# Reordering the second expert layer: copies and conversions among the next pair's sums, later ring loads, separate sum buffers

## Chip, core and metric

The program runs on one of the eight cores of a Trainium2 chip. The metric is the device time of one execution in microseconds (us). A core has TensorE (PE in the views; its weight loads are PEld), VectorE (DVE), ScalarE (ACT), GpSimd (POOL) and SyncE (SP). Each runs its own instructions in order and waits at semaphores for the others. Here SP issues nearly all DMAs.

## What is computed

Causal attention with a forget gate, over 4 batches, 8 heads, 576 positions and 64 dimensions, then two dense layers over the 2304 tokens:

```python
x = attention(q, k, v, f)               # 2304 x 512
h = x @ w_in                            # 512 -> 2048
y = softplus(h) @ w_out                 # 2048 -> 512
gate = sigmoid(y @ w_gate)              # 512 -> 1536
out = (gate * (y @ w_val)) @ w2_out     # 1536 -> 512
```

Everything is float32. Each product is made of three matmuls on a high and a low part of both operands, so every operand is first split: ACT casts the high part, DVE subtracts it from the source to get the low part.

## The kernel before

There are three stages. `Attention` is not touched. `Moe1` is the softplus layer: five tiles of tokens, sixteen blocks per tile; block `fc` is 12 matmuls for `h`, the softplus, the split into `gh` and `gl`, and 12 matmuls into `oX` and `oY`, one block behind. `Moe2` is the gated layer: tiles of 512, 512, 512, 512 and 256 tokens and 12 units per tile. An even unit k makes the gate, the odd one after it the value, and the two are a pair.

A unit of `Moe2` for a 512-token tile (`hidden`, from line 807) multiplies 2x2 blocks by Strassen's scheme, seven products of six matmuls. In PE's order they are A11, S2, A12, S1, A22, S3, S4. They go into four PSUM buffers in turn (tags `s` and `t`, two each; the trace names the tiles `h_A` and `h_S`). A22 reuses the `t` buffer of S2, so it waits until DVE has read S2 (line 831). That needs ACT's copy `p1` of A11 (line 830, tile `L`). DVE makes five more sums (lines 832 to 839). Then ACT applies the sigmoid (line 841, tile `bh`), or DVE multiplies by the gate (line 843, tile `bl`). After an odd unit, `parts` (line 862) splits the product into `gh` and `gl` for two blocks, f = 0 and 1. `output` (line 874) adds these blocks' products into `zX` and `zY`, in the two units that follow. When a tile's last block is in, `leave` (line 890) copies the four sums `zX`, `zY` out and stores them. The next tile's first `output` writes the same PSUM.

Weights reach `Moe2` through DRAM. During `Moe1`, `Sums` forms the Strassen sums of the weights and stores them: high parts through the buffers `sh0` and `sh1`, low parts `l` (lines 679 to 683). `load` (line 724) reads one unit's weights, seven DMAs of 256 KB, into a ring of four places. `load_out` reads `w2_out`. `step` (line 764) prepares the next tile's tokens: it loads `yT` into `r` and `bl` (line 785), then ACT and DVE split them (lines 779, 780) and make their Strassen sums.

The order is written out by hand: each engine executes what the Python code emits, in that order. On SP a DMA waits until the buffer is free, and until the eighth DMA before it has landed. `extra1` and `after` (in the main function) set where `Moe2`'s first loads stand among `Moe1`'s last blocks: before the change, `m2.load()` is called in blocks 10 to 13 of the last tile.

Of the kernel before, what the change touches and what calls it, by code (L numbers as in the profile page):

```python
# [9 lines left out]
F32 = mybir.dt.float32  # L10
F32R = mybir.dt.float32r
# [10 lines left out]
class Attention:  # L22
# [391 lines left out]
    def run(self, others):  # L414

        edge = {0: self.START, self.NP - 1: self.END}
        ops = [(self.PERIOD * p + edge.get(p, {}).get(op, r), i, p, op) for p in range(self.NP)
               for i, (op, r) in enumerate(self.WHEN.items()) if p or op[0] not in self.FIRST]
        ops += [(t, -1, i, f) for i, (t, f) in enumerate(others)]
        for t, i, p, op in sorted(ops, key=lambda x: x[:3]):  # L420
            if i < 0:
                op()
            else:
                getattr(self, op[0])(self.R.setdefault(p, {}), p, *op[1:])
# [110 lines left out]
def three(nc, ps, terms, start, stop):  # L535

    n = len(terms)
    for i, (ah, al, bh, bl) in enumerate(terms):
        nc.tensor.matmul(ps, ah, bh, start=start and i == 0, stop=False)  # L539
        nc.tensor.matmul(ps, ah, bl, start=False, stop=False)  # L540
        nc.tensor.matmul(ps, al, bh, start=False, stop=stop and i == n - 1)  # L541


def block(w, i):
    return w[:, 128 * i:128 * i + 128]
# [90 lines left out]
class Sums:  # L636
# [11 lines left out]
    def add(self, lane, sums, names, srcs):  # L648

        for n in names:  # L650
            self.d[n] = self.dr.tile([4 if sums else 1, 2, 128, 512], F32, name="sd_%s%d" % n)
        self.lanes[lane].append((sums, names, srcs))
# [52 lines left out]
class Moe2:  # L705
# [6 lines left out]
    def __init__(self, nc, FC, yT, out, S, chain, ps, slot, zs):  # L712
# [3 lines left out]
        self.n = self.NT * 2 * self.J  # L716
        self.acc, self.g, self.x, self.loaded = {}, {}, {}, 0

    def get(self, name, i):
        if (name, i) not in self.cache:  # L720
            self.cache[name, i] = self.slot(name, i)
        return self.cache[name, i]
# [91 lines left out]
    def hidden(self, k):  # L814
        t, r = divmod(k, 2 * self.J)
        gate = r % 2 == 0
        if self.plain(t):
            return self.hidden_plain(k, t, gate)
        nc = self.nc
        A, B = self.weights(k), self.tokens(t)  # L820
        C = self.chain("G" if gate else "V", k)
        p1, u2, u3, u4 = (self.chain(n, k) for n in ("p1", "u2", "u3", "u4"))
        c = lambda i: C[:, 256 * i:256 * i + 256]

        def product(tag, a, b):
            ps = self.ps.tile([128, 512], F32, tag=tag, bufs=2, name=f"h{k}_{a}")[:, 0:256]
            three(nc, ps, [(block(A[a][0], kk), block(A[a][1], kk), *B[b][kk]) for kk in range(2)], True, True)
            return ps
        add = nc.vector.tensor_add
        nc.scalar.copy(p1, product("s", "A11", "x11"))  # L830
        add(u2, product("t", "S2", "T2"), p1)  # L831
        add(c(0), product("s", "A12", "x21"), p1)
        p5 = product("t", "S1", "T1")
        add(u4, p5, u2)
        p4 = product("t", "A22", "T4")
        add(u3, product("s", "S3", "T3"), u2)  # L836
        add(c(3), p5, u3)
        add(c(2), p4, u3)
        add(c(1), product("s", "S4", "x22"), u4)  # L839
        if gate:  # L840
            nc.scalar.activation(C, C, AF.Sigmoid)  # L841
        else:
            nc.vector.tensor_mul(C, C, self.chain("G", k))  # L843

    def hidden_plain(self, k, t, gate):
        nc = self.nc
        w = [[self.get(f"ring{k % self.RING}", 2 * f + p) for p in range(2)] for f in range(2)]
        x = [[self.get(f"x{t % 2}", 2 * (c // 2) + p)[:, 256 * (c % 2):256 * (c % 2) + 256] for p in range(2)]
             for c in range(4)]
        C, G = self.chain("G" if gate else "V", k), self.chain("G", k)  # L850
        for f in range(2):
            b = self.ps.tile([128, 512], F32, tag="ts"[gate], bufs=2, name=f"h{k}_{f}")[:, 0:256]
            three(nc, b, [(block(w[f][0], c), block(w[f][1], c), *x[c]) for c in range(4)], True, True)
            o = slice(256 * f, 256 * f + 256)
            if gate:
                nc.scalar.activation(C[:, o], b, AF.Sigmoid)
            else:
                nc.vector.tensor_mul(C[:, o], b, G[:, o])

    def parts(self, k):  # L860
        nc, m, n = self.nc, self.chain("V", k), self.TILES[k // (2 * self.J)][1]
        for f in range(2):
            s = m[:, n * f:n * f + n]
            h, l = (self.chain("g" + p, k)[:, 0:n] for p in "hl")
            nc.scalar.copy(h, s)  # L865
            nc.vector.tensor_sub(l, s, h)
            self.g[k // 2, f] = h, l


    def output(self, i, f):  # L870

        nc = self.nc
        t, j = divmod(i, self.J)
        o, n = self.TILES[t]
        first, last = (j, f) == (0, 0), (j, f) == (self.J - 1, 1)
        if first:
            X = self.ps.tile([128, 1024], F32, tag="X", name=f"zX{t}")
            Y = self.ps.tile([128, 1024], F32, tag="Y", name=f"zY{t}")
            self.acc[t] = [X[:, 0:512], X[:, 512:1024], Y[:, 0:512], Y[:, 512:1024]]
        gh, gl = self.g.pop((i, f))  # L880
        wh, wl = (self.get("w2", 2 * (2 * j + f) + p) for p in range(2))
        for b in range(n // 128):
            a = self.acc[t][b]
            nc.tensor.matmul(a, block(gh, b), wh, start=first, stop=False)  # L884
            nc.tensor.matmul(a, block(gh, b), wl, start=False, stop=False)  # L885
            nc.tensor.matmul(a, block(gl, b), wh, start=False, stop=last)
        if last:
            for b in range(2):
                self.leave(t, b)

    def leave(self, t, b):
        nc, z, o = self.nc, self.zs[b], self.TILES[t][0] + 128 * b
# [10 lines left out]
            self.load_out(k + 2)  # L903
        self.load()

    def run(self, first, before):
        for k in range(first, self.n + 2):
            if k < self.n:
                self.unit(k)
            i = (k - 2) // 2  # L910
            if k == first:
                before()
            elif i >= self.J and i % self.J == 0 and k % 2 == 0:

                for b in (2, 3):
                    self.leave(i // self.J - 1, b)
            if i >= 0:
                self.output(i, k % 2)
            if k < self.n and k % 2:
                self.parts(k)  # L920
# [11 lines left out]
def kernel(ctx: ExitStack, tc, q, k, v, f, w_in, w_out, w_gate, w_val, w2_out, out):  # L932
    nc = tc.nc
# [28 lines left out]
    with ExitStack() as actx:  # L962
# [6 lines left out]
        m1 = []  # L969
# [14 lines left out]
    chain, m1 = m1  # L984
    xb = pool("xb", 1, **later)
    x1.pools.append(xb)
    wc = pool("wc", 1, **later)
    W.add_slots(wc, tags("c", 4 * FC1 - 2 * EARLY - 2 * MORE))
    W.limit = 2 * FC1
    last = m1.n - FC1  # L990
    raws, ws, highs = [], [], [wc.tile([128, 512], F32R, name=f"sh{i}") for i in range(2)]
    S = Sums(nc, W, dr, raws, ws, highs, chain)
    gv = [(n, j, w) for j in range(FC2 // 2) for n, w in (("g", w_gate), ("v", w_val))]
    for i, (n, j, w) in enumerate(gv):
# [19 lines left out]
    box = {}  # L1014
# [18 lines left out]
    def buffers(name, k):  # L1033

        if name in ("gh", "gl"):
            return chain.tile([128, 512], F32R, tag=name, name=f"{name}{k}", bufs=2)
        if name == "r1":
            return raw.tile([128, 512], F32, tag="xr", name=f"r1_{k}")
        if name in ("p1", "u2", "u3", "u4"):
            if "L" not in box:  # L1040
                box["L"] = [chain.tile([128, 512], F32, tag="L", name=f"L2_{i}", bufs=2) for i in range(2)]
            i = ("p1", "u2", "u3", "u4").index(name)
            return box["L"][i % 2][:, 256 * (i // 2):256 * (i // 2) + 256]
        if "b" not in box:
            box["b"] = [xb.tile([128, 4, 448], F32R, tag="x" + w, name="b" + w)[:].bitcast(F32).rearrange(
                "p a b -> p (a b)") for w in "hl"]
        b = box["b"]["GqVr".index(name[0]) // 2]
        return b[:, 0:1024] if name in "GV" else b[:, 1024:1536]

    m2 = Moe2(nc, FC2, yT, out, S, buffers, ps, slot, ws)  # L1050
# [4 lines left out]
    def extra1(u):  # L1055
        t, fc = divmod(u, FC1)
        if u == FC1 - 1:
            fixed()
        if t and fc:
            if fc < 15:  # L1060
                S.step(0)
            if t < m1.NT - 1 or fc >= 4:
                S.step(1)
        if t == m1.NT - 1 and fc >= 5:
            if fc - 5 < m2.STEPS:
                m2.step(0, fc - 5)
            if fc >= 10 and fc < 14:
                m2.load()

    def after(i):  # L1070
        m2.load_out(0)
        m2.load_out(1)
        m2.unit(i)

    def rest():
        for d in (2, 3):
            m1.leave(m1.NT - 1, d)

    W.alone()
    W.tick(2)  # L1080
    m1.run(len(UNITS), pieces1, extra1, after)
    m2.run(m1.LAG, rest)


# [32 lines left out]
```

## Time and profile before

| | |
|---|---|
| three runs | 1073.56, 1077.10, 1076.71 us; median 1076.71 us |
| the profiled execution | 1076.53 us, of which the span from the first to the last instruction is 1074.7 us |
| PE busy | 1033.5 us, 96% of the span |
| DVE, ACT, POOL busy | 679.0, 452.6, 155.6 us |
| mean granted clock of TensorE | 0.988 |
| attention, the softplus layer, the gated layer | to about 300 us, to about 633 us, to the end |

All times below count from the start of the span. "Idle before" is an engine's own idle time just ahead of an instruction, with what ended it. A PE matmul is shown with a modelled end, so successive matmuls overlap in the rows; how many PE does in a time is read from their starts.

### The profile page before, as it was taken

The numbers are of one execution on the slowest core, as the hardware profiler recorded it, in microseconds if no ns is written. First come the engines' busy times: TensorE is split into PE (matmuls) and PEld (weight loads), VectorE is DVE, ScalarE is ACT, GpSimd is POOL, SyncE is SP. The second block draws the span as 40 slices with busy tenths as digits, with TensorE's granted clock in tenths as the row PEclk, the third lists the DMA queues.
The fourth block names the chain that finished last, engine by engine and source line by source line (L and its number), as shares of the span: only waits on it lengthen the run. The fifth ranks groups of instructions, "written<-read, shape, count | busy, mean of one in ns | idle before, by whom it ended". The sixth has DMA issues, their size and how long they took to land.

```text
span 1074.7 us, 17922 instructions
## 1 busy us (share of the span) xinstructions
PE 1033.5 (96%) x6376; PEld 925.0 (86%) x6376; DVE 679.0 (63%) x1453; ACT 452.6 (42%) x989; POOL 155.6 (14%) x158
## 2 busy tenths in 40 slices
PE   4989999989999999999999998999999999999998
PEld 3777888868889999999999988998999899989997
DVE  6898999978945755656646636655655656555421
ACT  4687888865644343343344432222212222122121
POOL 7656776550000000000000000000000000000000
PEclk8899999999999999999999999999999999999999
DMA  6354454455534654655643599988787887786481
GB/s 169 89 150 129 126 142 125 138 142 176 212 123 174 197 211 175 213 191 182 226 170 138 182 394 371 327 263 272 245 252 245 274 261 231 254 257 210 152 271 63
DMA packets 129493, 218.24 MB, mean 203 GB/s; under 512 B 16174, under 2 KB 46526, under 8 KB 129404
## 3 DMA queue, kind: packets, MB, share of 16 engines
q1 hardware_dynamic: 129244, 216.80, 62.3%
q8 instruction: 50, 0.82, 0.3%
q10 hardware_dynamic: 160, 0.30, 0.1%
q14 instruction: 39, 0.32, 0.1%
HBM read 171.21 MB, written 45.83 MB: 202 GB/s over the span
## 4 chain that ended last, share of the span: by engine, by line
PE 85%; DVE 7%; DMA 4%; ACT 2%; issue 2%; SPq 0%; POOL 0%; DVEq 0%; POOLq 0%; ACTq 0%
PE h L541 7%; PE h L539 7%; PE h L540 7%; PE s L220 5%; PE t L250 4%; PE x L322 4%; PE h_S L539 4%; PE h_S L541 4%; PE h_S L540 4%; PE h_A L539 3%; PE h_A L541 3%; PE h_A L540 3%; PE zX L884 2%; PE zX L885 2%; PE oY L539 2%; PE oY L541 2%
## 5 line engine op out<-in xcount | busy, mean ns | idle before, releaser
L541 PE MATMUL h<-xh,wi_l 128*128 128x448 f32 (+1 forms) x320 | 119.0, 372 | 0.0
L540 PE MATMUL h<-xl,wi_h 128*128 128x448 f32 (+1 forms) x320 | 119.0, 372 | 0.0
L539 PE MATMUL h<-xh,wi_h 128*128 128x448 f32 (+1 forms) x320 | 118.9, 372 | 0.0
L581 DVE TENSOR_TENSOR gl<-L,gh 128x448 fp32r<-128x448 f32 (+1 forms) x80 | 51.1, 638 | 102.6 <-ACT gh L580 102.4
L569 ACT ACTIVATE L<-h 128x448 f32<-128x448 f32 (+1 forms) x80 | 44.2, 552 | 148.6 <-PE h L541 144.9
L865 ACT CAST gh<-bl 128x512 fp32r<-128x512 f32 (+1 forms) x60 | 32.2, 577 | 142.8 <-DVE bl L843 120.5
L232 ACT ACTIVATE P<-P,m 128x128 f32<-128x128 f32 (+3 forms) x144 | 83.4, 583 | 13.0 <-DVE m L227 13.0
L540 PE MATMUL h_S<-x,ring 128*128 128x256 f32 x288 | 81.5, 283 | 0.0
L227 DVE CUSTOM_DVE_ANT_0 P<-s,mask 128x256 f32<-128x256 f32 (+3 forms) x144 | 70.8, 517 | 16.4 <-PE s L220 11.2
L539 PE MATMUL h_S<-x,ring 128*128 128x256 f32 x264 | 74.7, 283 | 0.0
L541 PE MATMUL h_S<-x,ring 128*128 128x256 f32 x264 | 74.7, 283 | 0.0
L841 ACT ACTIVATE bh<-bh 128x1024 f32<-128x1024 f32 x24 | 25.4, 1059 | 107.8 <-DVE bh L839 107.8
L250 PE MATMUL t<-ident,P 128*128 128x128 f32 x400 | 62.3, 293 | 8.6 <-DVE PTbl L272 5.6
L541 PEld LDWEIGHTS h<-xh,wi_l 128*128 128x128 f32 x320 | 60.1, 188 | 7.2
L539 PEld LDWEIGHTS h<-xh,wi_h 128*128 128x128 f32 x320 | 60.1, 188 | 7.1
L540 PEld LDWEIGHTS h<-xl,wi_h 128*128 128x128 f32 x320 | 60.1, 188 | 7.1
L250 PEld LDWEIGHTS t<-ident,P 128*128 128x128 f32 x400 | 47.0, 147 | 21.1 <-DVE PTbl L272 7.1
L681 DVE TENSOR_TENSOR l<-fw,sh 128x512 fp32r<-128x512 f32 x60 | 40.7, 686 | 37.9 <-ACT sh L680 37.9
L540 PEld LDWEIGHTS h_S<-x,ring 128*128 128x128 f32 x288 | 55.2, 192 | 0.0
L540 PE MATMUL h_A<-x,ring 128*128 128x256 f32 x192 | 54.3, 283 | 0.0
L539 PE MATMUL h_A<-x,ring 128*128 128x256 f32 x168 | 48.5, 289 | 5.2 <-DVE L L831 4.0
L836 DVE TENSOR_TENSOR L<-h_S,L 128x256 f32<-128x256 f32 x48 | 20.4, 425 | 49.7 <-PE h_S L541 49.7
(233 smaller groups left out, 3065.3 us busy)
## 6 DMA issues: line engine op xcount, KB each, us to landing
ring<-sd_g SPq DMA_DIRECT2D x192, 256.0 KB
ring<-sd_v SPq DMA_DIRECT2D x192, 256.0 KB
raw_wi<-in_moe_w_in_dram SPq DMA_DIRECT2D x16, 512.0 KB
raw_wo<-in_moe_w_out_dram SPq DMA_DIRECT2D x16, 512.0 KB
fraw<-in_moe_w_gate_dram SPq DMA_DIRECT2D x12, 512.0 KB
fraw<-in_moe_w_out_dram SPq DMA_DIRECT2D x12, 512.0 KB
sd_g<-sh SPq DMA_DIRECT2D x24, 256.0 KB
sd_g<-l SPq DMA_DIRECT2D x24, 256.0 KB
```

Source lines behind the costliest of these rows:

```text
L220: nc.tensor.matmul(ps[h][:, 0:N], L[o], r[o, 0:N], start=j == 0, stop=j == n - 1)
L227: self.nc.vector.tensor_tensor_reduce(P, src, mask, -0.125, 3e38, op0=ALU.add, op1=ALU.min, accum_out=R["m"][:, t:t + 1])
L232: self.nc.scalar.activation(P, P, AF.Exp, bias=R["m"][:, t:t + 1], scale=-1.0, accum_out=R["sum"][:, t:t + 1])
L250: nc.tensor.transpose(ps[:, 128 * n:128 * n + 128], R["P"][:, o:o + 128], self.ident)
L322: nc.tensor.matmul(R["acc%d" % h][:, o:o + n], v, t[:, col:col + n], start=j == 0 and w == 0, stop=j == 1 and w == 1)
L539: nc.tensor.matmul(ps, ah, bh, start=start and i == 0, stop=False)
L540: nc.tensor.matmul(ps, ah, bl, start=False, stop=False)
L541: nc.tensor.matmul(ps, al, bh, start=False, stop=stop and i == n - 1)
L569: nc.scalar.activation(g, ph, AF.Softplus)
L581: nc.vector.tensor_sub(gl, s, gh)
L681: nc.vector.tensor_sub(l, w[n], h)
L865: nc.scalar.copy(h, s)
```

## The change

It has five parts. (1) In `parts` the second block's split goes onto a list `between[0]` and is emitted in the middle of the next unit, after the adds of lines 831 and 832. (2) The four `leave` of a tile go onto `between[0]` and `between[1]`, so they are emitted inside the next tile's unit: two after line 832, two after line 839. The last two copies of the softplus layer (`rest`) go the same way. (3) `m2.load()` is called in blocks 13, 14 and 15 and once in `after`, instead of blocks 10 to 13. (4) `p1` and `u2` to `u4` move from two `L` buffers of the softplus layer to `sh0` and `sh1`, buffers of `Sums`. (5) ACT's table for the sigmoid is loaded explicitly at the start of `after`.

```diff
--- before.py
+++ after.py
@@ -716,6 +716,8 @@
         self.n = self.NT * 2 * self.J
         self.acc, self.g, self.x, self.loaded = {}, {}, {}, 0
 
+        self.between = [[], []]
+
     def get(self, name, i):
         if (name, i) not in self.cache:
             self.cache[name, i] = self.slot(name, i)
@@ -830,6 +832,7 @@
         nc.scalar.copy(p1, product("s", "A11", "x11"))
         add(u2, product("t", "S2", "T2"), p1)
         add(c(0), product("s", "A12", "x21"), p1)
+        self.other(0)
         p5 = product("t", "S1", "T1")
         add(u4, p5, u2)
         p4 = product("t", "A22", "T4")
@@ -837,10 +840,16 @@
         add(c(3), p5, u3)
         add(c(2), p4, u3)
         add(c(1), product("s", "S4", "x22"), u4)
+        self.other(1)
         if gate:
             nc.scalar.activation(C, C, AF.Sigmoid)
         else:
             nc.vector.tensor_mul(C, C, self.chain("G", k))
+
+    def other(self, i):
+        for f in self.between[i]:
+            f()
+        self.between[i] = []
 
     def hidden_plain(self, k, t, gate):
         nc = self.nc
@@ -851,6 +860,7 @@
         for f in range(2):
             b = self.ps.tile([128, 512], F32, tag="ts"[gate], bufs=2, name=f"h{k}_{f}")[:, 0:256]
             three(nc, b, [(block(w[f][0], c), block(w[f][1], c), *x[c]) for c in range(4)], True, True)
+            self.other(f)
             o = slice(256 * f, 256 * f + 256)
             if gate:
                 nc.scalar.activation(C[:, o], b, AF.Sigmoid)
@@ -859,12 +869,18 @@
 
     def parts(self, k):
         nc, m, n = self.nc, self.chain("V", k), self.TILES[k // (2 * self.J)][1]
-        for f in range(2):
+
+        def part(f):
             s = m[:, n * f:n * f + n]
             h, l = (self.chain("g" + p, k)[:, 0:n] for p in "hl")
             nc.scalar.copy(h, s)
             nc.vector.tensor_sub(l, s, h)
             self.g[k // 2, f] = h, l
+        part(0)
+        if k + 1 < self.n:
+            self.between[0].append(lambda: part(1))
+        else:
+            part(1)
 
 
     def output(self, i, f):
@@ -885,8 +901,12 @@
             nc.tensor.matmul(a, block(gh, b), wl, start=False, stop=False)
             nc.tensor.matmul(a, block(gl, b), wh, start=False, stop=last)
         if last:
-            for b in range(2):
-                self.leave(t, b)
+            if t < self.NT - 1:
+                for b in range(4):
+                    self.between[b // 2].append(lambda b=b: self.leave(t, b))
+            else:
+                for b in range(n // 128):
+                    self.leave(t, b)
 
     def leave(self, t, b):
         nc, z, o = self.nc, self.zs[b], self.TILES[t][0] + 128 * b
@@ -903,17 +923,11 @@
             self.load_out(k + 2)
         self.load()
 
-    def run(self, first, before):
+    def run(self, first):
         for k in range(first, self.n + 2):
             if k < self.n:
                 self.unit(k)
             i = (k - 2) // 2
-            if k == first:
-                before()
-            elif i >= self.J and i % self.J == 0 and k % 2 == 0:
-
-                for b in (2, 3):
-                    self.leave(i // self.J - 1, b)
             if i >= 0:
                 self.output(i, k % 2)
             if k < self.n and k % 2:
@@ -988,7 +1002,7 @@
     W.add_slots(wc, tags("c", 4 * FC1 - 2 * EARLY - 2 * MORE))
     W.limit = 2 * FC1
     last = m1.n - FC1
-    raws, ws, highs = [], [], [wc.tile([128, 512], F32R, name=f"sh{i}") for i in range(2)]
+    raws, ws, highs = [], [], [wc.tile([128, 512], F32R, tag=f"sh{i}", name=f"sh{i}") for i in range(2)]
     S = Sums(nc, W, dr, raws, ws, highs, chain)
     gv = [(n, j, w) for j in range(FC2 // 2) for n, w in (("g", w_gate), ("v", w_val))]
     for i, (n, j, w) in enumerate(gv):
@@ -1038,7 +1052,7 @@
             return raw.tile([128, 512], F32, tag="xr", name=f"r1_{k}")
         if name in ("p1", "u2", "u3", "u4"):
             if "L" not in box:
-                box["L"] = [chain.tile([128, 512], F32, tag="L", name=f"L2_{i}", bufs=2) for i in range(2)]
+                box["L"] = [wc.tile([128, 512], F32, tag=f"sh{i}", name=f"L2_{i}") for i in range(2)]
             i = ("p1", "u2", "u3", "u4").index(name)
             return box["L"][i % 2][:, 256 * (i // 2):256 * (i // 2) + 256]
         if "b" not in box:
@@ -1064,22 +1078,21 @@
         if t == m1.NT - 1 and fc >= 5:
             if fc - 5 < m2.STEPS:
                 m2.step(0, fc - 5)
-            if fc >= 10 and fc < 14:
+            if fc >= 13:
                 m2.load()
 
     def after(i):
+        nc.scalar.preload_act_table_set("sigmoid_and_others")
+        m2.load()
         m2.load_out(0)
         m2.load_out(1)
         m2.unit(i)
-
-    def rest():
-        for d in (2, 3):
-            m1.leave(m1.NT - 1, d)
+        m2.between = [[lambda: m1.leave(m1.NT - 1, 2), lambda: m1.leave(m1.NT - 1, 3)], []]
 
     W.alone()
     W.tick(2)
     m1.run(len(UNITS), pieces1, extra1, after)
-    m2.run(m1.LAG, rest)
+    m2.run(m1.LAG)
 
 
 # ---- launch: one core; inputs and outputs as the reference has them ----
```

PE's rows are the same, in the same order. Three places elsewhere are moved.

On SP, at the end of the softplus layer, from the token load of the first tile on. `sd_g<-sh` and `sd_g<-l` are stores of `Sums`; `ring` are weight loads for the gated layer. Before:

```order
L785 DMA bl<-yT 128x512
L733 DMA ring_0_6593<-sd_g_3411 128x512
L733 DMA ring_1_6595<-sd_g_3411 128x512
L733 DMA ring_2_6597<-sd_g_3411 128x512
L733 DMA ring_3_6599<-sd_g_3411 128x512
L733 DMA ring_4_6601<-sd_g_3411 128x512
L733 DMA ring_5_6603<-sd_g_3411 128x512
L739 DMA ring_6_6605<-sd_g_3411 128x2x256
L682 DMA sd_g_3433<-sh_3409 128x512
L683 DMA sd_g_3433<-l_7_1_1_6638 128x512
L733 DMA ring_0_6649<-sd_v_3412 128x512
```

The same place after the change:

```order
L787 DMA bl<-yT 128x512
L682 DMA sd_g_3433<-sh_3409 128x512
L683 DMA sd_g_3433<-l_7_1_1_6624 128x512
L682 DMA sd_g_3433<-sh_3409 128x512
L683 DMA sd_g_3433<-l_7_1_2_6706 128x512
L735 DMA ring_0_6716<-sd_g_3411 128x512
L735 DMA ring_1_6718<-sd_g_3411 128x512
```

Four stores, of which the last pair is made in block 13, now stand ahead of the first ring load. From that load to the token load `bl<-yT` of the second tile, later in the same queue, there are 61 DMAs before and 57 after.

On ACT, the units 1 to 3 of the gated layer, with `L608` the late copy of the softplus layer's `oY`. Before:

```order
L830 COPY L_0_6859<-h_A_6946 128x256
L608 COPY fw_4131<-oY_6209 128x448
L865 CAST gh_7019<-bl 128x512
L865 CAST gh_7023<-bl 128x512
L830 COPY L_0_6859<-h_A_7030 128x256
L841 ACTIVATE bh<-bh 128x1024
L779 CAST y1h<-bl 128x512
L830 COPY L_0_6859<-h_A_7118 128x256
```

After:

```order
L832 COPY L_0_6860<-h_A_6947 128x256
L608 COPY fw_4131<-oY_6209 128x448
L876 CAST gh_7020<-bl 128x512
L832 COPY L_0_6860<-h_A_7027 128x256
L876 CAST gh_7051<-bl 128x512
L845 ACTIVATE bh<-bh 128x1024
L781 CAST y1h<-bl 128x512
L832 COPY L_0_6860<-h_A_7119 128x256
```

The second block's cast goes behind `p1` of unit 2. In both orders the cast `y1h<-bl` of the newly loaded tokens stands ahead of `p1` of unit 3 (the last row).

On DVE, the first unit of the second tile, with `zX` and `zY` the copies of the first tile's sums. Before:

```order
L843 TENSOR_TENSOR bl<-bl,bh 128x1024
L893 COPY fw_4128<-zX_7099 128x512
L866 TENSOR_TENSOR gl_8067<-bl,gh_8066 128x512
L866 TENSOR_TENSOR gl_8071<-bl,gh_8070 128x512
L831 TENSOR_TENSOR L_1_6860<-h_S_8085,L_0_6859 128x256
L832 TENSOR_TENSOR bh<-h_A_8093,L_0_6859 128x256
L834 TENSOR_TENSOR L_1_6860<-h_S_8101,L_1_6860 128x256
```

After:

```order
L847 TENSOR_TENSOR bl<-bl,bh 128x1024
L877 TENSOR_TENSOR gl_8064<-bl,gh_8063 128x512
L833 TENSOR_TENSOR L_1_6861<-h_S_8078,L_0_6860 128x256
L834 TENSOR_TENSOR bh<-h_A_8086,L_0_6860 128x256
L913 COPY fw_4128<-zX_7100 128x512
L877 TENSOR_TENSOR gl_8099<-bl,gh_8098 128x512
L837 TENSOR_TENSOR L_1_6861<-h_S_8102,L_1_6861 128x256
```

The copy of `zX` and one subtraction go from ahead of the first two sums to behind them. On ACT the copy of `zY` likewise goes from behind the sigmoid to ahead of it.

## Rows read from the trace of the kernel before

**Rows 1.** PE's waits from 560 us to the end: engine, line, releaser: total, times, longest

```profile
PE h_A L539 <- DVE L L831: 4.3, 5, 2.5
PE zY L884 <- ACT fw L893: 3.3, 3, 1.1
PE h_A L539 <- ACT L L569: 1.1, 1, 1.1
```

**Rows 2.** Timeline of PE, units 0 to 3: start, duration, line, tiles, [idle before <-releaser]

```profile
633.23 0.39 PE L539 MATMUL h_A<-x,ring 128*128 128x256 f32 x1 [1.07 <-ACT L L569]
...
634.65 0.28 PE L541 MATMUL h_S<-x,ring 128*128 128x256 f32 x1
635.04 0.38 PE L539 MATMUL h_A<-x,ring 128*128 128x256 f32 x1
...
650.39 0.39 PE L539 MATMUL h_A<-x,ring 128*128 128x256 f32 x1 [2.54 <-DVE L L831]
...
658.03 0.28 PE L540 MATMUL h_S<-x,ring 128*128 128x256 f32 x1
658.15 0.28 PE L541 MATMUL h_S<-x,ring 128*128 128x256 f32 x1
659.37 0.38 PE L539 MATMUL h_A<-x,ring 128*128 128x256 f32 x1 [0.95 <-DVE L L831]
```

**Rows 3.** Timeline of SP, from the last sums' stores to the second tile's token load

```profile
608.12 0.38 SPq L682 DMA_DIRECT2D sd_v<-sh  x1
...
610.19 2.82 SPq L733 DMA_DIRECT2D ring<-sd_g  x6
...
651.34 0.53 SPq L785 DMA_DIRECT2D bl<-yT  x1
```

**Rows 4.** Timeline of ACT in the same stretch

```profile
618.94 0.57 ACT L580 CAST gh<-L 128x448 fp32r<-128x448 f32 x1
...
631.81 0.62 ACT L680 CAST sh<-fw 128x512 fp32r<-128x512 f32 x1 [7.34 <-DMA sd_g<-sh]
...
656.84 0.62 ACT L779 CAST y1h<-bl 128x512 fp32r<-128x512 f32 x1 [2.07 <-DMA bl<-yT]
```

**Rows 5.** Timeline of DVE in the same stretch

```profile
620.44 0.69 DVE L681 TENSOR_TENSOR l<-fw,sh 128x512 fp32r<-128x512 f32 x1 [0.28 <-ACT sh L680]
...
658.90 0.42 DVE L831 TENSOR_TENSOR L<-h_S,L 128x256 f32<-128x256 f32 x1
```

**Rows 6.** Stretches: length, busy time of the engines, granted clock, DMA share, GB/s

```profile
605.00:610.00 5.00, 5.00 (x26) 4.54 (x25) 3.59 (x7) 2.19 (x5) 0.00 (x0) 1.00 0.44 165
...
640.00:650.00 10.00, 7.85 (x66) 7.64 (x64) 5.84 (x12) 3.29 (x7) 0.00 (x0) 1.00 1.04 382
```

**Rows 7.** Two stretches in attention, the same columns: PE first

```profile
89.50:92.90 3.40, 1.45 (x10) 0.97 (x11) 3.37 (x11) 1.03 (x4) 0.01 (x1) 1.00 0.95 283
92.93:96.34 3.41, 3.41 (x17) 2.64 (x17) 1.94 (x5) 2.83 (x9) 0.64 (x1) 0.50 0.08 20
```

**Rows 8.** Timeline of PE, unit 8 and the first change of tiles

```profile
698.86 0.39 PE L539 MATMUL h_A<-x,ring 128*128 128x256 f32 x1 [0.28 <-DVE L L831]
...
745.58 0.28 PE L541 MATMUL h_S<-y1l,ring 128*128 128x256 f32 x1
745.82 0.39 PE L539 MATMUL h_A<-y1l,ring 128*128 128x256 f32 x1
...
750.72 0.50 PE L884 MATMUL zY<-w,gh 128*128 128x512 f32 x1 [1.09 <-ACT fw L893]
```

**Rows 9.** Timeline of DVE and ACT at the first change of tiles

```profile
744.14 1.29 DVE L866 TENSOR_TENSOR gl<-bl,gh 128x512 fp32r<-128x512 f32 x2 [1.17 <-ACT gh L865]
...
749.02 0.68 DVE L893 COPY fw<-zY 128x512 f32<-128x512 f32 x1
...
750.10 0.57 ACT L893 COPY fw<-zY 128x512 f32<-128x512 f32 x1
```

## The prediction

> **What bounds the kernel now.** I read the table of engines first: PE is busy 96% of the span and its order is unchanged, so the time can only change where PE waits, or runs at another clock. Next come PE's waits in the second half [rows 1]: 8.7 us in nine waits. Three are for ACT's copy of `zY`, five for DVE's line 831, one for the softplus. In the timeline of PE [rows 2] the first four stand close together, in units 0, 2 and 3 of the gated layer; three show 1.07, 2.54 and 0.95 us of idle time, and the one at 635.04 shows as a late start. A shown wait costs more than it shows. Successive matmuls start 0.12 us apart (658.03, 658.15), and the next, at 659.37, starts 1.10 us later than that pace, where 0.95 us is shown; so 0.16 us is added for each (at 635.04 the start is 0.27 late). The matmul after a wait runs about 0.10 us longer (0.38 against 0.28). The four together cost 1.07 + 2.54 + 0.95 + 3 x 0.16 + 0.27 + 4 x 0.10 = 5.7 us.
>
> Then I ask what ends these waits. In the timeline of ACT [rows 4] the cast `sh` stood 7.34 us idle until the store of its buffer had landed, and the softplus of the last block is behind it. Later the cast `y1h` waited for the token load `bl`, and unit 3's `p1` is behind that. PE went on at 659.37, 2.53 us after `y1h` began. Both releasers are DMAs. In the timeline of SP [rows 3] the first ring load is issued at 610.19 and `bl` at 651.34. By the stretches [rows 6] the 16 DMA engines went from a share of 0.44 before 610 us to 1.04 at 640 to 650 us, with 382 GB/s. The queue is full, so landing times are set by how many DMAs stand ahead. There are 61 DMAs from the first ring load to `bl`, in 41.15 us, which is 0.675 us each.
>
> **The later ring loads (part 3).** The stores no longer stand behind ring loads, so the 7.34 us wait of ACT goes, and with it PE's waits in unit 0. What is late next is `bl`. The first ring load now stands behind the stores of block 13. In that block `gh` ends at 619.51 [rows 4], the cast takes 0.62 and the subtraction 0.69 us, which ended at 621.13 even with a short wait in front [rows 5]; the load follows at about 621.2, that is 11.0 us later than now. From there to `bl` stand 57 DMAs, four fewer.
>
> Before, `bl` had landed 46.65 us after the first ring load was issued (656.84 less 610.19). Taking off four DMAs at 0.675 leaves 43.95, so it lands at 665.15: the late bound. Before, the first ring load also had at least four DMAs ahead of it in flight, issued from 608.12 on [rows 3]; after, the queue is nearly empty at 621 us. That takes off up to 2.7 us more: 662.45, the early bound. I take 663.4, nearer the early one, since the empty queue is read from the order and from the idle share. PE goes on 2.53 us later, at 665.93. Without any wait it would be at that matmul at 659.37 - 5.31 (the four waits) - 0.30 (three restarts) = 653.76. So one wait of 12.2 us, 12.3 with its restart, takes the place of 5.7: +6.6 us (5.6 to 8.3 by the two bounds).
>
> The Trainium skill (DMA: Bandwidth & Descriptors, Specifications) states about 358 GB/s as a core's share of its memory. By that figure 57 loads of 256 KB take an estimated 41.7 us rather than 57 x 0.675 = 38.5, and the sum would be 3.2 us higher. The trace disagrees with the figure (382 GB/s).
>
> **The clock after that wait.** PE has had no wait near 12 us in this half of the trace. The nearest rows are in attention [rows 7]: after a stretch in which PE was busy 1.45 of 3.40 us, the granted clock was 0.50 (1.2 instead of 2.4 GHz) for 3.41 us with PE busy throughout. That cost about half of 3.41 us, 1.7 us. I add 1.7. The bounds are 0, if it is granted in full when PE starts again, and 3.4, two such stretches. A gain is excluded, since it ran at 1.00 before.
>
> The Trainium skill (TensorE: Matmul & The Clock Gate, Part 1) says the same from the other side: half rate is what an idle engine gets, and activity releases it. By the rule the loss is certain and only its length open; by the mean clock of 0.988 alone one would have set it to nothing, and the sum at 1.7 us less.
>
> **Units 0 to 2 (parts 4 and 5, the split of unit 1, the late copies).** The table load moves from behind unit 0's sums to before `p1`. `p1` now has to wait until the last store from `sh0` has landed. In unit 2 one cast instead of two stands ahead of `p1`. I cost all of this at nothing: unit 3's wait ends at a landing, and a us won or lost in units 0 to 2 is only taken from that wait. If that cover is gone, the wait of 2.54 us in unit 2 [rows 2] shrinks to about 0.6, since one of its two casts and one copy are out of the way.
>
> **Moved splits (part 1).** In unit 8 of three tiles, DVE's line 831 stands behind two subtractions and the token sums, and PE waits 0.28 us (three of the five waits) [rows 1, 8]: 0.28 + 0.16 + 0.10 = 0.54. One subtraction takes 1.29 / 2 = 0.65 us [rows 9] and now stands behind line 832, so the wait goes: -1.6 us for three. In all other even units the moved subtraction lies in the time in which DVE waits for the fourth product. If that cover were too short, PE would lose up to 0.65 us in each.
>
> **Moved copies (part 2).** At each of three changes of tiles PE loses 0.12 + 0.10 us at 745.82 behind the copy of `zX`. Then it loses 1.09 + 0.16 = 1.25, and 0.11 for the restart, at `zY` [rows 8], because ACT's copy stands behind the sigmoid and begins at 750.10 [rows 9]. Together 4.7 us for three. After, ACT's copy runs in the middle of the unit. DVE's copy of `zY` still stands behind the last sum and ends at 749.70 [rows 9], where PE could begin at 750.72 - 1.25 = 749.47: about 0.27 + 0.10 us stay, 1.1 for three. Net -3.6 us. The bounds are 0 (`zY` as late as now) and -4.7. The stores of these copies now stand before the next ring load on SP, at most 1.5 us in its way, in a stage in which the ring is three units ahead.
>
> **Sum.** The profiled execution took 1076.53 us, 0.18 below the median of 1076.71. 1076.53 + 6.6 + 1.7 - 1.6 - 3.6 = 1079.6 us. A change of 0.3% (3.2 us), about what a measurement of this kernel can tell from none, begins at 1073.5 and at 1079.9.
>
> **Rivals.** (a) Not slower: the queue carries the 57 DMAs faster, and `bl` lands at 660. For it: the early bound has no stray delay in it. Against it: 0.675 us was held for 41 us at a full share. The wait then costs 660 + 2.53 - 653.76 + 0.10 = 8.9, net +3.2; with -5.2 and the clock kept, 1074.5 us. It decides at a landing of about 662 with the clock kept, and 660.3 with it halved; earlier than that, the gains win.
>
> (b) Much faster: the token load is no bound, because its landing before 651 us lets unit 3 pass. Then -5.7 + 0.6 - 5.2 = -10.3, 1066.2 us. For it: ACT's wait for `bl` was only 2.07 us [rows 4]. Against it: at 651 the queue would have had to do 57 DMAs in 30 us.
>
> (c) Slower: the changes of tiles keep their wait, since `zY` as one tile is released only by DVE's copy behind the last sum, and two more instructions on DVE in that unit push this back. For it: that copy ends after PE is ready. Against it: DVE had idle time in front of line 836. Only the 1.6 us are won: 1083.2 us.
>
> **Chances.** The forecast 0.55, from 1077 to 1082 by its own bounds, half of it on each side of 1079.9: 0.27 same, 0.28 slower. (a) 0.16: 0.13 same, 0.03 faster. (b) 0.09, faster. (c) 0.20: 0.02 same, 0.18 slower. Faster 0.12, same 0.42, slower 0.46. The range leaves out (b) below and the clock's 3.4 us on top of (c) above: 1073.5 to 1084.5.
>
> **What will show it.** The first ring load issued near 621 us; `y1h` starting on ACT near 663 us after a long wait for `bl`; one idle time of about 12 us on PE in unit 3, and none in units 0 and 8; a stretch at clock 0.50 just behind it; waits of about 0.3 us at `zY`. I am wrong if `bl` lands before 660 us, if PE waits in units where it did not before, or if the clock stays at 1.00 after the wait.

## The result and the profile after

Six runs took 1081.67 to 1087.54 us, median 1083.16; beside them the kernel before took 1071.35 to 1077.10, median 1074.8. The ratio is 1.0086 [1.0059, 1.0112], so the change costs about 9.2 us. The profiled execution took 1082.45 us (span 1080.6, mean granted clock 0.982, PE busy 1028.1 us).

PE's waits in the second half of the kernel after, in the columns of [rows 1]:

```profile
PE h_A L539 <- DVE L L833: 14.6, 2, 13.6
PE zY L900 <- ACT fw L913: 5.1, 3, 1.7
```

Two waits in the place of five for DVE's first sum, with more than three times their time; the softplus wait is gone; and the three for `zY` are there still, longer than the 3.3 us of before. PE's timeline, in the columns of [rows 2]:

```profile
625.24 0.28 PE L539 MATMUL h_A<-x,ring 128*128 128x256 f32 x1
...
641.85 0.39 PE L539 MATMUL h_A<-x,ring 128*128 128x256 f32 x1 [0.96 <-DVE L L833]
...
663.52 0.58 PE L539 MATMUL h_A<-x,ring 128*128 128x256 f32 x1 [13.64 <-DVE L L833]
...
757.14 0.50 PE L900 MATMUL zY<-w,gh 128*128 128x512 f32 x1 [1.72 <-ACT fw L913]
...
1075.73 0.39 PE L902 MATMUL zX<-w,gl 128*128 128x512 f32 x1
```

The first and last rows are the gated layer's first and last matmul. The same two of before:

```profile
630.57 0.28 PE L539 MATMUL h_A<-x,ring 128*128 128x256 f32 x1
...
1069.83 0.39 PE L886 MATMUL zX<-w,gl 128*128 128x512 f32 x1
```

From start to start the gated layer takes 439.26 us before and 450.49 after: +11.2. The two spans differ by 5.9 only, since this execution of the kernel after came to its gated layer 5.3 us sooner (the last section says where). I compare all kernels below by the length of the gated layer, each read from one profile, and by their ratios. The +11.2 of this pair lies within the ratio's interval, which is 6.3 to 12.0 us.

What ends the long wait, on SP (compare [rows 3]):

```profile
616.12 4.20 SPq L735 DMA_DIRECT2D ring<-sd_g  x6
...
655.44 0.41 SPq L787 DMA_DIRECT2D bl<-yT  x1
```

and on ACT, with the first change of tiles behind it (compare [rows 4, 9]):

```profile
660.99 0.62 ACT L781 CAST y1h<-bl 128x512 fp32r<-128x512 f32 x1 [14.77 <-DMA bl<-yT]
...
752.25 0.59 ACT L913 COPY fw<-zX 128x512 f32<-128x512 f32 x1 [2.07 <-DVE fw L913]
752.74 0.62 ACT L876 CAST gh<-bl 128x512 fp32r<-128x512 f32 x1
...
756.50 0.59 ACT L913 COPY fw<-zY 128x512 f32<-128x512 f32 x1 [3.14 <-DVE fw L913]
```

The token load lands 44.9 us after the first ring load was issued (660.99 less 616.12), where before it was 46.65. PE's wait follows 2.53 us behind the cast, as before. Stretches of the kernel after, in the columns of [rows 6]:

```profile
616.00:620.00 4.00, 4.00 (x22) 3.70 (x21) 1.30 (x4) 1.82 (x4) 0.00 (x0) 1.00 0.90 297
620.00:625.00 5.00, 5.00 (x26) 4.64 (x25) 1.51 (x3) 2.06 (x4) 0.00 (x0) 1.00 0.92 272
...
635.00:640.00 5.00, 5.00 (x43) 5.00 (x42) 3.94 (x8) 0.53 (x1) 0.00 (x0) 1.00 1.06 382
...
655.00:660.00 5.00, 0.00 (x0) 0.00 (x0) 0.00 (x0) 0.00 (x0) 0.00 (x0) 0.50 1.01 362
...
663.50:669.10 5.60, 5.58 (x22) 5.29 (x23) 3.11 (x7) 0.00 (x0) 0.00 (x0) 0.50 1.06 381
670.00:690.00 20.00, 20.00 (x143) 18.80 (x142) 12.46 (x27) 5.28 (x11) 0.00 (x0) 1.00 0.90 285
```

From 625 us on the queue is full, as before, but not in its first 9 us. The clock falls to 0.50 while PE is idle, and stays there for 5.6 us after PE has started again, in which it issues 22 matmuls.

So the 11.2 us come out as follows. Waits in units 0 to 3: 0.96 + 13.64 + 2 x 0.16 + 2 x 0.10 = 15.1 against 5.7, +9.4. The clock: half of 5.6, +2.8. Each `zY`: 1.72 + 0.16 + 0.11 = 1.99 for three, 6.0 against 4.7 with the `zX` part, +1.2. The three waits of unit 8: gone, -1.6. The sum is 11.8, which is 0.6 more than the 11.2 measured; that rest is not accounted for.

### The profile page after: what moved, and what is told of

Read it like the earlier page. It is cut to its first block, busy times and chain, and to the rows that moved or that the text cites. A ratio compares the mean times of both kernels' runs of the same rounds, so it can differ in the third digit from the quotient of the medians.

```text
span 1080.6 us, 17900 instructions
## 1 busy us (share of the span) xinstructions
PE 1028.1 (95%) x6376; PEld 925.3 (86%) x6376; DVE 679.3 (63%) x1453; ACT 454.7 (42%) x989; POOL 155.9 (14%) x158
## 4 chain that ended last, share of the span: by engine, by line
PE 83%; DVE 7%; DMA 5%; ACT 2%; issue 2%; SPq 1%; POOL 0%; DVEq 0%; POOLq 0%; ACTq 0%
PE h L540 7%; PE h L539 7%; PE h L541 7%; PE s L220 4%; PE t L250 4%; PE h_S L541 4%; PE h_S L539 4%; PE h_S L540 4%; PE x L322 4%; PE h_A L539 3%; PE h_A L541 3%; PE h_A L540 3%; PE zX L900 2%; PE zX L901 2%; PE zX L902 2%; PE oY L540 2%
## 5 line engine op out<-in xcount | busy, mean ns | idle before, releaser
L876 ACT CAST gh<-bl 128x512 fp32r<-128x512 f32 (+1 forms) x60 | 34.7, 580 | 170.5 <-DVE bl L847 143.3
L569 ACT ACTIVATE L<-h 128x448 f32<-128x448 f32 (+1 forms) x80 | 44.3, 554 | 144.4 <-PE h L541 133.2
```

The costliest lines, as they stand in the source:

```text
L569: nc.scalar.activation(g, ph, AF.Softplus)
```

## The experiments

My theory of the loss: the whole of it is the later ring (part 3), by one wait and the clock behind it, and what the moved copies (part 2) were to give did not come, because their new places bring a new wait. The rivals: the separate sum buffers (part 4) make the loss; or the clock costs nothing apart from the wait; or `zY` was held by the number of instructions on DVE and not by their order. All kernels compute the same output.

### x1: the token load ahead in the queue

```diff
         m2.load()
+        m2.step(1, 0)
         m2.load_out(0)
...
-        if t + 1 < self.NT and r >= 2:
+        if t + 1 < self.NT and r >= 2 and k != 2:
```

> The changed kernel, with one move: the second tile's token load (r and bl) is issued right behind the fourth ring load, 25 DMAs earlier in the queue. Theory (the late ring start puts the token load at the end of a full queue): bl lands about 26 x 0.68 = 17.7 us earlier, near 643 us, before ACT comes to it; the 13.6 us wait of PE in unit 3 goes, the clock stays at 1.00, and the time falls by 13.9 + 2.8 = 16 us or a little less, to about 1067 us, some 8 us below the kernel before. Rival (the wait is made by the new order on ACT and DVE, not by the queue): PE still waits over 10 us in unit 3 and the time stays near 1083. Rival (another DMA is as late): a wait of 5 us or more moves to unit 3 or 4 behind a ring load or a w load, and the time is 1073 to 1078.

Measured: 1075.26 us, ratio 1.0021 [1.0005, 1.0037]; gated layer 442.41. PE's waits, and its timeline in unit 8:

```profile
PE h_A L539 <- DVE L L833: 7.4, 2, 6.5
```

```profile
695.50 0.58 PE L539 MATMUL h_A<-x,ring 128*128 128x256 f32 x1 [6.46 <-DVE L L833]
```

The wait in unit 3 is gone, so it was the position of this load in the queue that made it. But half of it comes back 32 us later: now the second token load stands behind the ring's loads, and the queue still runs at a share of 1.06 from 670 to 690 us, where the kernel after had 0.90. Behind this wait, too, the clock is at 0.50:

```profile
695.50:698.43 2.93, 2.93 (x13) 2.93 (x14) 1.21 (x3) 0.00 (x0) 0.00 (x0) 0.50 1.05 372
```

I had expected the whole wait to be won and the clock to stay at 1.00. The second rival came nearest: its time was right, but it had the new wait in unit 3 or 4 and behind a load of weights. Here, moving one load ahead of the others passed the queue's delay on to the next load.

### x2: the copies apart

```diff
+                self.first = lambda: self.leave(t, 0)
+                self.between[0].append(lambda: self.leave(t, 1))
+                self.late = [lambda: self.leave(t, 2), lambda: self.leave(t, 3)]
...
         part(0)
+        if self.first:
+            self.first()
...
-            self.between[0].append(lambda: part(1))
+            self.between[0] += self.late[:1] + [lambda: part(1)] + self.late[1:]
```

DVE's copy of `zX` goes in front of the first sum, both copies of `zY` to the middle of the unit, DVE's ahead of the moved subtraction.

> The changed kernel, with the copies at the changes of tiles taken apart: DVE copies the first quarter of zX before line 833 (as in the kernel before), ACT's copies come behind p1, DVE's first copy of zY comes before the moved subtraction. Theory (ACT's copy waits for DVE's copy of the same PSUM tile, and DVE's chain in that unit is too long): zY is released about 3 us earlier, the three waits of 1.72 us at zY go, and the time is 3 x 1.98 = 5 to 6 us below the changed kernel, about 1077; the 13.6 us wait in unit 3 stays. Rival (the wait at zY is set by the last sum of the unit whatever stands in front): the waits stay above 1 us, and the time stays within 2 us of 1083.

Measured: 1077.0 us, 1.0026 [1.0011, 1.0041]; gated layer 442.90, 7.6 us less than the kernel after. PE's one line of waits of over 1 us in all, and ACT at the first change of tiles:

```profile
PE h_A L539 <- DVE L L834: 13.2, 2, 12.3
```

```profile
748.94 0.59 ACT L918 COPY fw<-zX 128x512 f32<-128x512 f32 x1 [0.21 <-DVE fw L918]
...
750.80 0.59 ACT L918 COPY fw<-zY 128x512 f32<-128x512 f32 x1 [0.75 <-DVE fw L918]
```

All of the `zY` waits go by order alone (6.0 us of the 7.6). The wait in unit 3 is 1.4 us shorter because the token load landed 43.5 us behind the first ring load, where the kernel after had 44.9. The same number of instructions runs on DVE, so the number was not the cause.

### x3, x4 and x9: the ring's place and the buffers apart

x3 is the changed kernel without parts 3 and 4:

```diff
-                box["L"] = [wc.tile([128, 512], F32, tag=f"sh{i}", name=f"L2_{i}") for i in range(2)]
+                box["L"] = [chain.tile([128, 512], F32, tag="L", name=f"L2_{i}", bufs=2) for i in range(2)]
...
-            if fc >= 13:
+            if fc >= 10 and fc < 14:
                 m2.load()
...
-        m2.load()
         m2.load_out(0)
```

> The changed kernel with parts 3 and 4 undone (ring loads in blocks 10 to 13, sums in the old L buffers); parts 1, 2 and 5 stay. Theory: bl lands near 657 us as in the kernel before, the four waits there cost 4 to 6 us together, no long wait and no half clock; the time is 11 to 13 us below the changed kernel at equal softplus stage, 1071 to 1076, within 3 us of the kernel before, with the waits of 1.7 us at zY still there and those of unit 8 gone. Rival (parts 1 and 2 make the long wait): PE still waits over 10 us in unit 3, and the time stays near 1083.

x4 is the kernel before with part 3 alone:

```diff
-            if fc >= 10 and fc < 14:
+            if fc >= 13:
                 m2.load()
...
     def after(i):
+        m2.load()
         m2.load_out(0)
```

> The kernel before with part 3 alone (ring loads in blocks 13, 14, 15 and in the first unit). Theory: bl lands 44 to 45 us after the first ring load, near 665 us; PE waits 12 to 14 us in unit 3 and runs about 5 us at half clock; unit 0's waits go, 1.09 us at zY and 0.28 us in unit 8 stay as before; the time is 9 to 12 us above the kernel before, 1084 to 1087. Rival (the long wait needs the moved splits or the new sum buffers): less than 3 us above the kernel before.

x9 is x3 without its first hunk: the sums stay in `sh0` and `sh1`, and only part 3 is undone.

> The changed kernel with part 3 alone undone: ring loads in blocks 10 to 13, the sums still in sh0 and sh1. It prices part 4 without the cover of the late ring. Theory: the last store from sh0 stands behind the ring loads and lands about 4 us after PE has finished A11 of unit 0 (in x3 it landed at 631.88, p1 began at 629.40), so p1 and PE wait 2.5 to 4 us more in unit 0 than in x3; a part of it comes back in the waits of units 2 and 3 (2.4 us in x3), so the gated layer is 0.5 to 3 us longer than in x3, and the time is within 4 us of the kernel before. Rival (the buffers cost nothing): as x3 within 0.5 us in the trace.

| | median us | ratio to before | gated layer us |
|---|---|---|---|
| before | | 1 | 439.26 |
| after | 1083.16 | 1.0086 [1.0059, 1.0112] | 450.49 |
| x3 | 1072.56 | 0.9993 [0.9977, 1.0010] | 439.01 |
| x4 | 1085.04 | 1.0098 [1.0072, 1.0125] | 449.90 |
| x9 | 1077.32 | 1.0030 [1.0008, 1.0052] | 442.79 |

PE's waits in x3, in x4, and in x9:

```profile
PE zY L900 <- ACT fw L913: 5.1, 3, 1.7
PE h_A L539 <- DVE L L833: 3.4, 3, 1.4
PE h_A L539 <- ACT L L569: 1.8, 1, 1.8
```

```profile
PE h_A L539 <- DVE L L831: 12.7, 5, 9.3
PE zY L884 <- ACT fw L893: 3.3, 3, 1.1
```

```profile
PE h_A L539 <- DVE L L833: 5.4, 3, 3.7
PE h_A L539 <- ACT L L569: 1.1, 1, 1.1
```

Part 3 alone makes the kernel before slower by 10.5 us, as much as the whole change. Its wait in unit 3 is shorter than that of the kernel after (9.3 us, where I had expected 12 to 14), because PE comes to it later: unit 2 keeps its wait of 2.5 us, and behind that one, too, the clock is at 0.50 for 3.4 us. It has the stretch at half clock after unit 3's wait as well, of the same 5.6 us. Both stretches:

```profile
646.91:650.32 3.41, 3.41 (x17) 3.36 (x16) 1.39 (x5) 0.00 (x0) 0.00 (x0) 0.50 1.06 387
...
665.20:670.80 5.60, 5.59 (x22) 5.30 (x23) 3.11 (x7) 0.00 (x0) 0.00 (x0) 0.50 1.06 382
```

In the kernel before, the same wait of 2.54 us left the clock at 1.00:

```profile
650.39:655.00 4.61, 4.61 (x29) 4.20 (x30) 2.12 (x6) 1.06 (x1) 0.00 (x0) 1.00 1.05 370
```

Without part 3 the loss goes, but nothing is won: in x3 the cast `sh` waits 7.89 us for a store again, and `zY` costs 1.2 us more than before, about what unit 8 gives. No run undoes part 1 or part 5 alone. The rival on the buffers has a part that does not show with the late ring: with the ring early, `sh0` and `sh1` cost 3.8 us (x9 less x3; the ratios' intervals just overlap, so this rests on the two profiles). The first sum's copy on ACT waits for a store from them:

```profile
634.00 0.37 ACT L832 COPY L<-h_A 128x256 f32<-128x256 f32 x1 [2.65 <-DMA sd_g<-sh]
```

That adds only 1.3 us to PE's waits (5.4 + 1.1 against 3.4 + 1.8). The larger part is the clock, which is at 0.50 for 5.6 us behind the wait of 3.69 us:

```profile
634.90:640.50 5.60, 5.60 (x23) 5.43 (x24) 2.20 (x6) 0.85 (x1) 0.00 (x0) 0.50 0.86 306
```

I had expected 0.5 to 3 us. In the kernel after, part 4 costs nothing, as forecast, but not for the reason given: nothing had to be covered by the wait in unit 3, since the same copy started at 626.16 us as soon as A11 was there, after 0.70 us of idle time for PE and none for a store.

### x5: PE kept busy in the wait

```diff
         p5 = product("t", "S1", "T1")
+        if k == 3:
+            for _ in range(16):
+                three(nc, p5, [(block(A["S1"][0], kk), block(A["S1"][1], kk), *B["T1"][kk]) for kk in range(2)], True, True)
```

Unit 3's product S1 is computed 17 times: 96 more matmuls, at 4.40 / 36 = 0.122 us each (row below) 11.7 us of work in the place of the wait.

> The changed kernel, in which unit 3 computes its product S1 seventeen times instead of once into the same PSUM buffer (each a fresh start, so the sum is the same): 96 matmuls more, 96 x 0.12 = 11.5 us of PE work in the time in which PE waits for the token load. Theory (the end of that wait is set by the landing of bl, and the idle engine's clock falls): the wait shrinks to about 2 us, it ends at the same place, the clock stays at 1.00 and the 2.8 us lost at half clock come back: 2 to 3 us below the changed kernel though work is added. Rival (PE's work sets the time there, or the half clock costs nothing): as long as the changed kernel or longer, up to 11.5 us.

Measured: 1080.67 us, 1.0074 [1.0049, 1.0099]. PE's waits for the first sum, and the stretch that ran at 0.50 in the kernel after:

```profile
PE h_A L539 <- DVE L L833: 2.2, 2, 1.2
```

```profile
663.50:669.10 5.60, 4.40 (x36) 4.20 (x36) 2.92 (x8) 0.89 (x2) 0.00 (x0) 1.00 1.06 385
```

The stretch runs at 1.00. The gated layer is 446.98 us, 3.5 shorter than that of the kernel after, though 11.7 us of work were added: 0.9 because work and rest of the wait (11.7 + 1.2) come to less than 13.64 + 0.16, as the token load landed 34.8 us after the layer's first matmul and not 35.8, and 2.6 that fit the 2.8 us put down to the clock. The ratios' intervals overlap, so this size stands on the two profiles alone.

### x6: the split ahead of the copies

The four `leave` go onto the lists in `parts`, behind the moved `part(1)`, so that DVE's and ACT's copies come after the second split.

```diff
-                for b in range(4):
-                    self.between[b // 2].append(lambda b=b: self.leave(t, b))
+                self.late = [[lambda b=b: self.leave(t, b) for b in (0, 1)], [lambda b=b: self.leave(t, b) for b in (2, 3)]]
...
             part(1)
+        for i, fs in enumerate(self.late):
+            self.between[i] += fs
+        self.late = []
```

> The changed kernel, with the moved split standing ahead of the first two copies of a change of tiles on ACT and DVE, and nothing else moved. One look. Theory (DVE copies zX, ACT copies zX after it, only then casts gh, and DVE waits 1.17 us for that cast before it goes on to the unit's later sums): that idle time goes, the last sum and the copies of zY come about 1.2 us earlier, and PE's waits at zY fall from 1.72 to about 0.5 to 0.9 us each; ACT's copy still begins after DVE's copy. Rival (it is only the serial pair of copies behind the last sum): the waits stay at 1.7 us.

Measured in one run: 1079.89 us; gated layer 445.70. PE's waits:

```profile
PE h_A L539 <- DVE L L834: 13.8, 2, 12.9
PE zY L904 <- ACT fw L916: 2.2, 3, 0.7
```

The `zY` waits fall from 1.72 to 0.75 us each, but do not go. DVE and ACT at the first change of tiles, in this kernel:

```profile
751.91 0.68 DVE L878 TENSOR_TENSOR gl<-bl,gh 128x512 fp32r<-128x512 f32 x1
...
755.19 0.68 DVE L916 COPY fw<-zY 128x512 f32<-128x512 f32 x1
```

```profile
755.91 0.59 ACT L916 COPY fw<-zY 128x512 f32<-128x512 f32 x1 [2.09 <-DVE fw L916]
```

and DVE in the kernel after:

```profile
751.54 0.68 DVE L913 COPY fw<-zX 128x512 f32<-128x512 f32 x1
753.39 0.69 DVE L877 TENSOR_TENSOR gl<-bl,gh 128x512 fp32r<-128x512 f32 x1 [1.17 <-ACT gh L876]
755.46 0.41 DVE L842 TENSOR_TENSOR bh<-h_S,L 128x256 f32<-128x256 f32 x1
755.79 0.68 DVE L913 COPY fw<-zY 128x512 f32<-128x512 f32 x1
```

This tells two parts of the wait apart. ACT's copy of `zX` begins only when DVE's has ended (751.54 + 0.68 = 752.22, then 752.25 on ACT), and `gh` is queued behind it on ACT; so DVE stands 1.17 us for `gh`, and the unit's later sums with it. That is gone in x6, and about 1 us of the wait with it. The other part stays: ACT's copy of `zY` begins only when DVE's has ended (755.19 + 0.68 = 755.87, then 755.91). The layer is 4.8 us shorter than that of the kernel after: 2.9 of them are the three waits, the rest is the wait in unit 3, 0.76 us shorter here, and the half clock behind it, which lasts 3.3 us and not 5.6.

### x7, x8 and x10: what the parts can give

x7 is x3 with the copies of x2. x8 is x7 with the ring's loads earlier, and x10 is x8 with x1's token load:

```diff
-            if fc >= 10 and fc < 14:
+            if fc in (7, 8, 10, 13):
                 m2.load()
```

> The changed kernel with parts 3 and 4 undone and the copies taken apart as in x2. Theory (the two costs are independent and add): the waits at zY go as in x2, the long wait as in x3, and the gated layer is 5.9 us shorter than in x3: about 1067 us, 0.5 to 0.6% below the kernel before. Rival (what is won at zY is lost again at the full queue later): within 0.2% of the kernel before.

> As x7, with the ring's four loads in blocks 7, 8, 10 and 13 of the last tile instead of 10 to 13. Theory (the first tile of the gated layer lives on what is loaded before it, since its units take as much as the queue carries): two units' weights move into a time in which the queue has room, the 7 us wait of ACT for the store of sh shrinks, bl lands earlier, and the waits of PE in units 0 to 3 (over 5 us together) mostly go: 3 to 5 us below x7. Rival (the loads only push the stores and the first tile's tokens back): a wait appears in the softplus layer's blocks 8 to 12, and it is no faster than x7.

> x8 with the second tile's token load moved ahead as in x1. Theory: bl lands before ACT comes to it, unit 3's wait of 1.35 us goes, unit 2's of 0.95 us stays (it is ACT's cast ahead of p1); since less debt is left in the queue than in x1, unit 8 waits under 1 us: 0 to 1.5 us below x8, so about 1063. Rival (as in x1 the debt is only paid later): a wait of 1 to 3 us in unit 8, and no gain on x8.

| | median us | ratio to before | gated layer us |
|---|---|---|---|
| x7 | 1067.86 | 0.9951 [0.9937, 0.9965] | 433.67 |
| x8 | 1064.01 | 0.9924 [0.9899, 0.9949] | 429.64 |
| x10 | 1062.58 | 0.9896 [0.9866, 0.9926] | 427.98 |

PE's waits of over 0.5 us in all in the second half of x7, x8 and x10:

```profile
PE h_A L539 <- DVE L L834: 4.0, 3, 2.0
PE h_A L539 <- ACT L L569: 1.9, 1, 1.9
```

```profile
PE h_A L539 <- DVE L L834: 2.3, 2, 1.3
```

```profile
PE h_A L539 <- DVE L L834: 1.0, 1, 1.0
```

x8 moves loads to where the queue has room. From 588 to 610 us, before:

```profile
588.00:610.00 22.00, 22.00 (x108) 19.99 (x107) 14.90 (x29) 11.05 (x21) 0.00 (x0) 1.00 0.34 128
```

and in x8:

```profile
588.00:610.00 22.00, 22.00 (x110) 20.38 (x110) 12.33 (x24) 9.65 (x18) 0.00 (x0) 1.00 0.93 327
```

The loads made there are out of the way of the last stores (`sh` waits 0.86 us, where [rows 4] has 7.34) and of the tokens. Each step takes a wait from PE and shortens the gated layer. x7 is faster than before, and x10 than x7; x8's interval overlaps both its neighbours', so its two steps rest on the profiles. x10 is the best version, 1.0% faster than before and 1.9% than the change.

## Why the forecast was right in sign and too small

The forecast was slower than before by 3.1 us, within 1073.5 to 1084.5; measured were about 9.2. The mechanism of the loss was right, and two terms were too small. The step that failed outright is "Moved copies (part 2)". That the median of 1083.16 us lies in the range is partly luck: the range starts from 1076.53 us and ends 8.0 above it, and beside the kernel after the one before took 1074.8.

**The wait of unit 3: +6.6 forecast, +9.4 measured.** The first ring load was 9.1 us before the first matmul of unit 0, within 0.3 of the place forecast. The load of the tokens then landed 44.9 us behind it; I had taken 42.2, and my late bound was 43.95. (The 660.99 us of this trace are not an early landing, since its gated layer began 5.3 us sooner: counted from the layer's first matmul it is 35.8 us, where the forecast had 32.8.) I had chosen the early side because the queue is nearly empty when the ring starts. No run bears that out. In the four other kernels with the late ring the same 57 DMAs took 43.5 (x2), 43.8 (x4), 44.1 (x5) and 44.3 us (x6), so the late bound was about right, and up to 1.4 of the 2.7 us missed is the spread between profiles. The queue was slow at first: against 382 GB/s, the stretches 616 to 620 and 620 to 625 us moved too little by 4 x (1 - 297/382) + 5 x (1 - 272/382) = 2.3 us. But it was so before as well, with DMAs in flight ahead: 610 to 615 and 615 to 620 us ran at 317 and 343 GB/s, too little by 1.4 us. What makes the start slow was not tried. The Trainium skill (DMA: Bandwidth & Descriptors, Specifications) gives about 358 GB/s for a core, and by it the forecast would have been 3.2 us higher and so closer; but the trace does not bear it out, since the queue, once full, ran at 382 again. Its mean from 616.12 to 660.99 us was 358 GB/s too, but that is a mean of stretches between 272 and 392.

**The clock: +1.7 forecast, +2.8 measured**, within its bounds of 0 to 3.4. After this idle time the half clock lasted 5.6 us, not the 3.41 of attention. The Trainium skill (TensorE: Matmul & The Clock Gate, Part 1) holds that an idle engine gets half rate and activity releases it; the trace agrees, with 0.50 in the idle stretch from 655 to 660 us and 1.00 in x5, whose PE never stood for more than 1.7 us in the gated layer. How long the half clock lasts after the wait does not follow from the length of the wait, so the size of this term was open: PE ran 2.9 us at 0.50 behind 6.46 us of waiting (x1), 3.3 behind 12.88 (x6), 5.6 behind 3.69 (x9), and behind 2.54 us 3.4 in x4 and none in the kernel before. With x6's 3.3 us the 1.7 would have come out.

**Units 0 to 2: nothing forecast, nothing measured**, with unit 2's wait at 0.96 where about 0.6 was named. The cover was not needed: no store held unit 0. x9 shows what such a store costs where the ring is early, 3.8 us, most of it in clock.

**Unit 8: -1.6 forecast, and the three waits are gone.** The 1.6 us are their price by the rows of before; no run measures part 1 alone.

**The copies: -3.6 forecast, +1.2 measured.** I let ACT's copy of `zY` run in the middle of the unit, and only DVE's count. But the program makes ACT's copy wait for DVE's copy of the same PSUM tile (the two write different buffers and share no other tile; no run gave the halves tiles of their own). The waits of ACT in the kernel before have it:

```profile
ACT fw L893 <- DVE fw L893: 30.5, 5, 7.3
```

I had read PE's waits and not this line of ACT's. With it the copies are a chain: DVE's, then ACT's, then whatever stands behind ACT's. The change puts `gh` there, and behind `gh` DVE's subtraction and the sums of the unit. So rival (c), with a chance of 0.20, was nearest: `zY` keeps its wait. Two more instructions on DVE were its reason; x2, with the same instructions, shows that their order does it. It had +6.7 us, with `zY` at no change, 1.2 us too good, and the terms of the wait and the clock as small as above.

Rival (a) asked for a landing about 3 us earlier than forecast, and (b) for one before 651 us; the trace has neither.

## What to carry to other kernels

A load that is made later moves all that stands behind it in its queue: find the last transfer that an engine will need, count the DMAs ahead of it, and look for a stretch with room in the queue before (x8) rather than let one load pass another in a full queue (x1); once there was room, that too helped, by 1.7 us in the profile of x10. Before moving instructions, read the waits of every engine that takes part in them, also those that cost nothing yet, since two copies of one tile may be a chain. A wait of TensorE can be paid twice, the second time in clock: here 13.64 us of waiting and then 5.6 us at 0.50, but also, in x9, 3.69 us of waiting and then the same 5.6.

## What was not expected of the hardware

The softplus layer, which the change does not touch in its middle, runs at one of two paces at the same granted clock of 1.00. From 420 to 480 us, before and then after:

```profile
420.00:480.00 60.00, 60.00 (x292) 54.51 (x291) 35.28 (x65) 25.32 (x46) 0.00 (x0) 1.00 0.65 230
```

```profile
420.00:480.00 60.00, 60.00 (x297) 55.35 (x296) 35.86 (x66) 27.87 (x51) 0.00 (x0) 1.00 0.63 222
```

292 matmuls against 297 in the same time with PE busy throughout. Fourteen blocks of that layer take 69.44 us in the profiles of before, x5 and x7, and 68.25 to 68.3 in those of after, x2, x3 and x8, whatever was changed. The slower pace begins within the layer: at about 340 us a block takes 4.86 or 4.87 us in every profile; from about 395 us on it takes 4.96 in before, x5 and x7, from a later place in x4, x6, x9 and x10, and nowhere for long in the others. From its first block to the gated layer's first matmul the layer takes 403.0 us in the profile of before and 398.7 in that of after. These are 4.3 of the 5.3 us by which the two stood apart when the gated layer began; the other 1.0 had come up in attention. The cause stays open.
